# First mixing in one float32 matmul per group, and the last 64 keys of the values as one matmul per pair of heads

## Chip, cores and metric

The kernel runs on one core of a Trainium2 chip. The metric is device time in microseconds from launch to end, as the median of several executions. Inputs and outputs are float32.

## What is computed

Attention with talking heads, four batches of 12 heads, 448 positions and 64 channels a head, followed by a two-layer MLP without bias. `w_pre` mixes the heads of the scores before the softmax, `w_post` those of the probabilities behind it.

```python
scores = (1.0 / np.sqrt(64)) * np.matmul(q, k.transpose(0, 1, 3, 2))
scores = np.einsum('bhij,hg->bgij', scores, w_pre)
scores = scores - np.max(scores, axis=-1, keepdims=True)
attn = np.exp(scores)
attn = attn / (np.sum(attn, axis=-1, keepdims=True) + 1e-09)
attn = np.einsum('bhij,hg->bgij', attn, w_post)
x = np.matmul(attn, v)          # then (B, S, H * D): 1792 rows of 768
h = x @ w_in                    # 768 -> 2048
out = np.maximum(0.01 * h, h) @ w_out
```

## The kernel before

**Tiling.** The queries of a batch are cut into chunks of 120 rows (the last has 88), 16 chunks in all. A chunk is worked on in groups of 10 rows by 12 heads, so that 120 partitions hold one group with all its heads; there are 12 groups in a chunk of 120 rows and 9 in one of 88, 180 in all. Three groups of four make the steps `s` of a chunk, and each of the 12 steps `t` of the loop over chunks does one piece of every stage, for three chunks at once.

**Stages.** `scores(n, h)` makes the scores of one head on TensorE (PE): two float32r passes, with a high and a low part of the queries, into PSUM tile `pss`, which ScalarE (ACT) copies to `st`. `regroup` sends them by DMA into tiles `rt` of 120 partitions (10 rows by 12 heads). `softmax(n, s, g)` is the first mixing: VectorE (DVE) casts `rt` to float32r (`rhi`), GpSimd (POOL) subtracts to get the remainder (`rlo`; DVE does it for every fourth group), and three float32r passes with the matrix `kpre`, itself in a high and a low part, add up in PSUM tile `psm`, which has two buffers. DVE takes the row maximum (`stat`), ACT the exponential and its sum (`et`). `mix` is the second mixing, in float32, with the matrix `kp` that holds `w_post` over the row sums: for each group and each 128 keys one matmul into `psa`, and for the last 64 keys, two of 64 columns each, even heads into the lower half of the partitions and odd heads into the upper (`half`). DVE and ACT copy `psa` to `at` and `half`. `values(n, pair)` multiplies with V for two heads at a time: head e of the pair writes partitions 64 e and up of `psx`, three matmuls over 128 keys and one over the last 64 for each head, so eight per pair. V stands twice for the last 64 keys, in the lower and in the upper half of the partitions, because the host repeats them.

**Beside it.** `prep_k` and `prep_q` split keys and queries into high and low parts on DVE, ACT and POOL; the keys of the next batch come in the third chunk of each batch. `Narrow` turns the 64-bit weights of the MLP into float32 (ACT, DVE, POOL), 36 pieces during the attention and 28 at the start of the MLP. `load_v` fetches the V of a batch into the one buffer there is. The MLP then goes through the four batches in 16 blocks of the hidden layer, `hidden` into `psh` and `project` into `pso`, with three float32r passes per product.

**What sets the order.** All instructions are recorded in the order of the loops, and a scheduler, which simulates a timeline of its own, puts each engine's queue in an order; each queue then runs strictly in that order. Tiles come from pools with a fixed number of buffers, and a buffer's next user waits for the last reader. All loads and stores but some of the results are issued by SyncE (SP).

Of the kernel before, what the change touches and what calls it, by code (L numbers as in the profile page):

```python
# [8 lines left out]
F32 = mybir.dt.float32  # L9
F32R = mybir.dt.float32r  # L10
# [11 lines left out]
ROWS = 10  # L22
# [10 lines left out]
def kernel(  # L33
# [10 lines left out]
    nc = tc.nc  # L44
    B, P, NJ, H, D = v.shape
    S = k.shape[3]
# [4 lines left out]
    RH = ROWS * H  # L51
    SLOTS = 3 * NJ
    HALF = SLOTS // 2
    HP = P // 2
# [13 lines left out]
    def pools(st, side):  # L68
        def pool(name, bufs, **kw):
            return st.enter_context(tc.tile_pool(name=name, bufs=bufs, side=side, **kw))  # L70
        return pool

    const = ctx.enter_context(tc.tile_pool(name="const", bufs=1, side="left"))
# [41 lines left out]
    pool = pools(left, "left")  # L115
    p_v = pool("v", 1)
    p_r = pool("r", SLOTS)
    p_rs = pool("rs", 3)
    p_e = pool("e", 2 * NJ + 1)
    p_st = pool("st", 2)  # L120
    p_at = pool("at", 2)
# [1 line left out]
    pool = pools(psum, "left")  # L123
# [3 lines left out]
    pool = pools(right, "right")  # L127
# [4 lines left out]
    p_c = pool("c", 1)  # L132
    ps_s = pool("ps_s", 3, space=PSUM)

    kw_t, k_t, q_t, v_t, s_t, r_t, rs_t, e_t, kp_t, at_t, xo_t = ({} for _ in range(11))

    def load_k(b, h):
        t = p_raw.tile([P, S], F32, tag="k", name="kraw", bufs=6)
# [34 lines left out]
    def load_v(b):  # L173
        t = p_v.tile([P, NJ, H, D], F32, tag="v", name="vt")
        nc.sync.dma_start(t, v[b])
        v_t[b] = t

    def scores(n, h):
# [20 lines left out]
    def softmax(n, s, g):  # L199
        sg = chunks[n][3][s]  # L200
        kk = sg[g][1] * H
        if g == 0:
            e_t[n, s] = [], p_st.tile([RH, 3, NJ], F32, tag="st", name="stat")
        es, st = e_t[n, s]
        e = p_e.tile([RH, S], F32, tag="e", name="et")
        es.append(e)
        raw = r_t.pop((n, s, g))
        hi = p_rs.tile([RH, S], F32R, tag="hi", name="rhi")
        lo = p_rs.tile([RH, S], F32R, tag="lo", name="rlo")
        nc.vector.tensor_copy(hi[:kk], raw[:kk])  # L210
        (nc.vector if g == 3 else nc.gpsimd).tensor_sub(lo[:kk], raw[:kk], hi[:kk].bitcast(F32))  # L211
        ps = ps_m.tile([RH, 512], F32, tag="m", name="psm")
        for i, (w, x) in enumerate(((1, hi), (0, lo), (0, hi))):
            nc.tensor.matmul(ps[:kk, :S], kpre[w][:kk, :sg[g][1], :], x[:kk], start=i == 0, stop=i == 2)  # L214
        nc.vector.tensor_reduce(st[:kk, 0, g:g + 1], ps[:kk, :S], axis=AX.X, op=ALU.max, negate=True)  # L215
        nc.scalar.activation(  # L216
            e[:kk], ps[:kk, :S], AF.Exp, bias=st[:kk, 0, g:g + 1], accum_out=st[:kk, 1, g:g + 1]
        )
        if g < len(sg) - 1:
            return  # L220
        kp = p_st.tile([RH, NJ, H, ROWS], F32, tag="kp", name="kp")
        kp_t[n, s] = kp
        full = sum(r == ROWS for _, r in sg)
        for a, z, kk in ((0, full, RH), (full, len(sg), sg[-1][1] * H)):
            if a < z:
                rs = st[:kk, 2, a:z]
                nc.vector.tensor_scalar_add(rs, st[:kk, 1, a:z], 1e-9)
                nc.vector.reciprocal(rs, rs)
                nc.vector.tensor_mul(  # L229
                    kp[:kk, a:z].rearrange("p g h r -> p g (h r)"),  # L230
                    kpost[:kk].rearrange("p h r -> p (h r)").unsqueeze(1).broadcast_to([kk, z - a, RH]),
                    rs.unsqueeze(2).broadcast_to([kk, z - a, RH]),
                )
# [38 lines left out]
    def values(n, pair):  # L272
        b, i0, m, _ = chunks[n]
        at, half = at_t[n]
        if pair % 3 == 0:
            xo_t[n] = ps_x.tile([P, 4, P], F32, tag="x", name="psx")
        ps = xo_t[n]
        for c in range(NJ):
            for e in range(2):
                h = 2 * pair + e  # L280
                up = slice(P) if c < NJ - 1 else slice(HP * e, HP * e + HP)
                nc.tensor.matmul(  # L282
                    ps[D * e:D * (e + 1), pair % 3, :m], v_t[b][up, c, h, :],
                    at[:, c, h, :m] if c < NJ - 1 else half[up, pair, :m], start=c == 0, stop=c == NJ - 1,
                )
        if pair % 3 == 2:
            xo = p_x.tile([P, 3, CHUNK], F32, tag="xo", name="xo")
            nc.vector.tensor_copy(xo[:, :, :m], ps[:, :3, :m])
            xo_t[n, pair // 3] = xo
# [92 lines left out]
    wt = const.tile([RH, 2, H], F32, name="wt")  # L382
    for i, w in enumerate((w_pre, w_post)):
        nc.sync.dma_start(wt[:, i, :], w.unsqueeze(0).broadcast_to([ROWS, H, H]))
    kraw = const.tile([RH, ROWS, H], F32, name="kraw")
    kpre = [const.tile([RH, ROWS, H], F32R, name=f"kpre{i}") for i in range(2)]
    kpost = const.tile([RH, H, ROWS], F32, name="kpost")
    nc.vector.tensor_copy(kraw, wt[:, 0, :].unsqueeze(1).broadcast_to([RH, ROWS, H]))
    nc.vector.tensor_copy(kpost, wt[:, 1, :].unsqueeze(2).broadcast_to([RH, H, ROWS]))
    for t, pat in ((kraw, ((H, ROWS), (0, H))), (kpost, ((0, H), (H, ROWS)))):  # L390

        nc.gpsimd.affine_select(
            t, t, pattern=[[-a, z] for a, z in pat], base=0, channel_multiplier=1, compare_op=ALU.is_ge, fill=0.0
        )
        nc.gpsimd.affine_select(
            t, t, pattern=[[a, z] for a, z in pat], base=H - 1, channel_multiplier=-1,
            compare_op=ALU.is_ge, fill=0.0,
        )

    nc.vector.tensor_copy(kpre[0], kraw)  # L400
    nc.vector.tensor_sub(kpre[1], kraw, kpre[0].bitcast(F32))

    with tc.issue_after(behind.ins):
        load_q(1)
# [1 line left out]
    regroup(0, 0, SLOTS)  # L406
    ctx.enter_context(tc.issue_after(last_dma[0].ins))
    load_v(0)
    prep_q(1, nc.vector.tensor_copy)
    for g in range(NJ):  # L410
        softmax(0, 0, g)
# [3 lines left out]
    for n in range(NCK):  # L415
        b = chunks[n][0]
# [3 lines left out]
        for t in range(SLOTS):  # L420
            s, c = divmod(t, NJ)
# [4 lines left out]
            if t == 0 and n % NB == 1 and n > 1:  # L426
                load_v(b)
# [11 lines left out]
            if t >= HALF and n:  # L439
                values(n - 1, t - HALF)  # L440
            nxt = (n, s + 1) if s < 2 else (n + 1, 0)
            if nxt[0] < NCK and c < len(chunks[nxt[0]][3][nxt[1]]):
                softmax(*nxt, c)
# [35 lines left out]
    for pair in range(NPAIR):  # L479
        values(NCK - 1, pair)  # L480
# [4 lines left out]
    pool = pools(mlp, "left")  # L485
# [3 lines left out]
    for i in range(1, n + 1):  # L489
        b, f = divmod(i, NF)  # L490
# [61 lines left out]
```

## Time and profile before

| | |
|---|---|
| time, median of 3 executions | 1090.8 us (1083.04 to 1097.96) |
| span of the profiled execution, its own time | 1094.2 us |
| PE busy | 1012.1 us, 93% |
| DVE busy | 839.4 us, 77% |
| POOL busy | 444.6 us, 41% |
| ACT busy | 424.6 us, 39% |
| first pass of the second MLP matmul | starts at 616.78 us |

The page and the trace are of one execution. PE's busy time covers a pass from its start to the end of its tail, and passes overlap, so a busy PE can still have room; the start-to-start distance of passes is the better measure of what one costs. "PEclk" is the TensorE clock that was granted, as a share of 2.4 GHz. Idle time of an engine stands with the one that ended it.

### The profile page before, as it was taken

The numbers are of one execution on the slowest core, as the hardware profiler recorded it, in microseconds if no ns is written. First come the engines' busy times: TensorE is split into PE (matmuls) and PEld (weight loads), VectorE is DVE, ScalarE is ACT, GpSimd is POOL, SyncE is SP. The second block draws the span as 40 slices with busy tenths as digits, with TensorE's granted clock in tenths as the row PEclk, the third lists the DMA queues.
The fourth block names the chain that finished last, engine by engine and source line by source line (L and its number), as shares of the span: only waits on it lengthen the run. The fifth ranks groups of instructions, "written<-read, shape, count | busy, mean of one in ns | idle before, by whom it ended". The sixth has DMA issues, their size and how long they took to land. (4 is left out here: it accounts for less than half of the span.)

```text
span 1094.2 us, 17821 instructions
## 1 busy us (share of the span) xinstructions
PE 1012.1 (93%) x6564; PEld 842.9 (77%) x6564; DVE 839.4 (77%) x1390; ACT 424.6 (39%) x951; POOL 444.6 (41%) x356
## 2 busy tenths in 40 slices
PE   4899889997899999999999988889999999999998
PEld 2576667775777767677768777779999999999997
DVE  6899887789888999768797599997556755565553
ACT  3664365644645646455552233332112211121111
POOL 5677764578565676546441165661000000000000
PEclk9999889998999999899999999999999999999999
DMA  5746533764354624536263455566333634353421
GB/s 184 282 161 194 190 110 119 234 198 156 119 171 158 240 70 154 177 112 216 100 230 89 136 181 177 178 179 214 102 116 103 205 102 116 104 163 101 116 89 63
DMA packets 93771, 167.11 MB, mean 153 GB/s; under 512 B 26740, under 2 KB 68724, under 8 KB 93172
## 3 DMA queue, kind: packets, MB, share of 16 engines
q1 hardware_dynamic: 91956, 163.23, 47.0%
q10 hardware_dynamic: 1728, 2.75, 0.7%
q8 instruction: 51, 0.84, 0.3%
q14 instruction: 36, 0.29, 0.1%
HBM read 103.82 MB, written 23.59 MB: 116 GB/s over the span
## 5 line engine op out<-in xcount | busy, mean ns | idle before, releaser
L211 POOL TENSOR_TENSOR rlo<-rt,rhi 120x448 fp32r<-120x448 f32 x144 | 175.3, 1221 | 141.6 <-DVE rhi L210 82.2
L332 DVE CAST wh<-wr 128x768 fp32r<-128x768 f32 x128 | 88.7, 695 | 138.3 <-PE psh L339 88.4
L256 PEld LDWEIGHTS psa<-kp,et 120*128 120x128 f32 (+2 forms) x1800 | 166.0, 174 | 35.7 <-issue 18.2
L256 PE MATMUL psa<-kp,et 120*128 120x120 f32 (+2 forms) x1800 | 179.8, 262 | 13.2 <-DVE kp L229 9.4
L216 ACT ACTIVATE et<-psm,stat 120x448 f32<-120x448 f32 x180 | 114.7, 639 | 152.7 <-DVE stat L215 151.3
L214 PE MATMUL psm<-rhi,kpre 120*120 120x448 f32 x360 | 149.5, 420 | 22.0 <-ACT et L216 21.7
L339 PE MATMUL pso<-gh,wl 128*128 128x448 f32 x384 | 141.7, 371 | 14.0 <-DVE wl L333 13.4
L339 PE MATMUL psh<-xh,wl 128*128 128x448 f32 x384 | 140.6, 366 | 3.5 <-DVE g L351 3.5
L339 PE MATMUL pso<-gl,wh 128*128 128x448 f32 x384 | 141.4, 368 | 0.0
L339 PE MATMUL pso<-gh,wh 128*128 128x448 f32 x384 | 141.4, 368 | 0.0
L339 PE MATMUL psh<-xh,wh 128*128 128x448 f32 x384 | 140.6, 366 | 0.0
L339 PE MATMUL psh<-xl,wh 128*128 128x448 f32 x384 | 140.4, 366 | 0.0
L350 ACT ACTIVATE t<-psh 128x448 f32<-128x448 f32 x64 | 34.8, 544 | 252.5 <-PE psh L339 243.2
L210 DVE CAST rhi<-rt 120x448 fp32r<-120x448 f32 x180 | 129.0, 717 | 2.3 <-DMA rt<-st 2.3
L215 DVE TENSOR_REDUCE stat<-psm 120x1 f32<-120x448 f32 x180 | 110.4, 614 | 26.4 <-PE psm L214 26.2
L333 DVE TENSOR_TENSOR wl<-wr,wh 128x768 fp32r<-128x768 f32 x128 | 123.8, 968 | 1.6
L187 ACT ACTIVATE st<-pss 120x448 f32<-120x448 f32 (+1 forms) x192 | 97.1, 551 | 57.4 <-PE pss L186 27.4
L282 PE MATMUL psx<-at,vt 128*64 128x120 f32 (+1 forms) x1152 | 109.0, 282 | 4.1 <-DVE at L264 2.7
L214 PEld LDWEIGHTS psm<-rhi,kpre 120*120 120x120 f32 x360 | 68.9, 191 | 47.0 <-ACT et L216 31.9
L282 PEld LDWEIGHTS psx<-at,vt 128*64 128x64 f32 x1152 | 68.0, 141 | 43.8 <-issue 31.5
L186 PE MATMUL pss<-kst,qlo 128*120 128x448 f32 (+1 forms) x192 | 82.3, 428 | 20.1 <-POOL kst L146 10.2
L339 PEld LDWEIGHTS pso<-gh,wl 128*128 128x128 f32 x384 | 72.9, 190 | 24.1 <-issue 14.5
(64 smaller groups left out, 1658.7 us busy)
## 6 DMA issues: line engine op xcount, KB each, us to landing
wr<-w_dram SPq DMA_DIRECT2D x114, 384.0 KB
rt<-st SPq DMA_DIRECT2D x176, 210.0 KB
craw<-in_w_moe SPq DMA_DIRECT2D x64, 384.0 KB
kraw<-in_k SPq DMA_DIRECT2D x48, 224.0 KB
qraw<-in_q SPq DMA_DIRECT2D x11, 720.0 KB
w_dram<-w SPq DMA_DIRECT2D x36, 192.0 KB
vt<-in_v SPq DMA_DIRECT2D x4, 1536.0 KB
xr<-x_dram SPq DMA_DIRECT2D x24, 224.0 KB
```

The costliest lines, as they stand in the source:

```text
L186: nc.tensor.matmul(ps[:m, :S], w[:, h, :m], k_t[b, h], start=i == 0, stop=i == 1)
L187: nc.scalar.activation(s_t[n][:m, h, :], ps[:m, :S], AF.Copy, scale=scale)
L210: nc.vector.tensor_copy(hi[:kk], raw[:kk])
L211: (nc.vector if g == 3 else nc.gpsimd).tensor_sub(lo[:kk], raw[:kk], hi[:kk].bitcast(F32))
L214: nc.tensor.matmul(ps[:kk, :S], kpre[w][:kk, :sg[g][1], :], x[:kk], start=i == 0, stop=i == 2)
L215: nc.vector.tensor_reduce(st[:kk, 0, g:g + 1], ps[:kk, :S], axis=AX.X, op=ALU.max, negate=True)
L216: nc.scalar.activation(e[:kk], ps[:kk, :S], AF.Exp, bias=st[:kk, 0, g:g + 1], accum_out=st[:kk, 1, g:g + 1])
L256: nc.tensor.matmul(ps[p0:p0 + np, w * g:w * g + nh * r], es[g][:r * H, c * P:c * P + np], kp[:r * H, g, h::step, :r], start=True, stop=True,)
L282: nc.tensor.matmul(ps[D * e:D * (e + 1), pair % 3, :m], v_t[b][up, c, h, :], at[:, c, h, :m] if c < NJ - 1 else half[up, pair, :m], start= ...
L332: nc.vector.tensor_copy(hi, raw)
L333: nc.vector.tensor_sub(lo, raw, hi.bitcast(F32))
L339: nc.tensor.matmul(ps, w[a][:, c * P:(c + 1) * P], x[e], start=first and j == 0, stop=last and j == 2)
```

## The change

The first mixing becomes one float32 matmul per group, straight from the regrouped tile `rt` and with a float32 `kpre`; the cast, the subtraction, their tiles and the split of `kpre` go. In the values, V's last block is made block-diagonal: in the half of the partitions that belongs to the even head, the columns of the odd heads are cleared, and the other way round, by two POOL instructions behind each load of V. One matmul over all 128 partitions and 128 columns then gives both heads of a pair their last 64 keys. It comes first in the pair and opens the sum; the six matmuls over 128 keys follow.

```diff
@@ pools, load_v @@
-    p_rs = pool("rs", 3)
...
         nc.sync.dma_start(t, v[b])
+        for e in range(2):
+            nc.gpsimd.memset(t[HP * e:HP * (e + 1), NJ - 1, 1 - e::2, :], 0.0)
@@ softmax @@
         raw = r_t.pop((n, s, g))
-        hi = p_rs.tile([RH, S], F32R, tag="hi", name="rhi")
-        lo = p_rs.tile([RH, S], F32R, tag="lo", name="rlo")
-        nc.vector.tensor_copy(hi[:kk], raw[:kk])
-        (nc.vector if g == 3 else nc.gpsimd).tensor_sub(lo[:kk], raw[:kk], hi[:kk].bitcast(F32))
         ps = ps_m.tile([RH, 512], F32, tag="m", name="psm")
-        for i, (w, x) in enumerate(((1, hi), (0, lo), (0, hi))):
-            nc.tensor.matmul(ps[:kk, :S], kpre[w][:kk, :sg[g][1], :], x[:kk], start=i == 0, stop=i == 2)
+        nc.tensor.matmul(ps[:kk, :S], kpre[:kk, :sg[g][1], :], raw[:kk], start=True, stop=True)
@@ values @@
-        for c in range(NJ):
+        nc.tensor.matmul(
+            ps[:, pair % 3, :m], v_t[b][:, NJ - 1, 2 * pair:2 * pair + 2, :], half[:, pair, :m],
+            start=True, stop=False, skip_group_check=True,
+        )
+        for c in range(NJ - 1):
             for e in range(2):
                 h = 2 * pair + e
-                up = slice(P) if c < NJ - 1 else slice(HP * e, HP * e + HP)
                 nc.tensor.matmul(
-                    ps[D * e:D * (e + 1), pair % 3, :m], v_t[b][up, c, h, :],
-                    at[:, c, h, :m] if c < NJ - 1 else half[up, pair, :m], start=c == 0, stop=c == NJ - 1,
+                    ps[D * e:D * (e + 1), pair % 3, :m], v_t[b][:, c, h, :], at[:, c, h, :m],
+                    start=False, stop=c == NJ - 2, skip_group_check=True,
                 )
@@ constants @@
-    kpre = [const.tile([RH, ROWS, H], F32R, name=f"kpre{i}") for i in range(2)]
+    kpre = const.tile([RH, ROWS, H], F32, name="kpre")
...
-    nc.vector.tensor_copy(kpre[0], kraw)
-    nc.vector.tensor_sub(kpre[1], kraw, kpre[0].bitcast(F32))
```

With the instructions the scheduler's order changes too. On PE, in the values of the sixth chunk, this stood before (in brackets, the engines or DMA queues that an instruction waits for):

```order
L282 MATMUL psx<-at,vt 64x120 x6
L282 MATMUL psx<-half,vt 64x120 x2
L214 MATMUL psm<-rhi,kpre_251 120x448 [waits Activation_49]
L282 MATMUL psx<-at,vt 64x120 x6
L282 MATMUL psx<-half,vt 64x120 x2
L214 MATMUL psm<-rhi,kpre_251 120x448 [waits Activation_49]
L214 MATMUL psm<-rlo,kpre_250 120x448 [waits DVE_49]
L214 MATMUL psm<-rhi,kpre_250 120x448
```

And this stands there now; line numbers are four to eight lower from the first mixing on:

```order
L274 MATMUL psx<-half,vt 128x120 [waits DVE_49]
L281 MATMUL psx<-at,vt 64x120 x6
L210 MATMUL psm<-rt,kpre 120x448 [waits DMAHW3_49,Activation_49]
L274 MATMUL psx<-half,vt 128x120
L281 MATMUL psx<-at,vt 64x120
L252 MATMUL psa<-kp,et 128x120 [waits DVE_49,PE_49]
L252 MATMUL psa<-kp,et 128x120 x3
L281 MATMUL psx<-at,vt 64x120 x5
L210 MATMUL psm<-rt,kpre 120x448 [waits DMAHW4_49,Activation_49]
```

The last block of a pair stands in front of it instead of behind it, as one matmul of 128 partitions; the three passes of a first mixing are one matmul, and its wait for POOL or DVE is one for a DMA queue.

On DVE, in the third chunk, where the keys of the second batch are prepared, this stood before:

```order
L145 CAST kst<-kraw 128x448 [waits DMAHW1_49,PE_49]
L227 TENSOR_SCALAR stat<-stat 120x4 [waits Activation_49]
L215 TENSOR_REDUCE stat<-psm 120x1 [waits PE_49]
L210 CAST rhi<-rt 120x448 [waits Pool_49]
L228 RECIPROCAL stat<-stat 120x4 [waits DVE_49]
L145 CAST kst<-kraw 128x448 [waits DMAHW2_49,PE_49]
L145 CAST kst<-kraw 128x448 [waits DMAHW3_49,PE_49]
L211 TENSOR_TENSOR rlo<-rt,rhi 120x448 [waits DVE_49]
L229 TENSOR_TENSOR kp<-kpost,stat 120x480 [waits DVE_49]
L215 TENSOR_REDUCE stat<-psm 120x1 [waits PE_49]
```

And now:

```order
L223 TENSOR_SCALAR stat<-stat 120x4 [waits Activation_49]
L211 TENSOR_REDUCE stat<-psm 120x1 [waits DVE_49,PE_49]
L224 RECIPROCAL stat<-stat 120x4 [waits DVE_49]
L144 CAST kst<-kraw 128x448 [waits DMAHW2_49,PE_49]
L225 TENSOR_TENSOR kp<-kpost,stat 120x480 [waits DVE_49]
L260 COPY at<-psa 128x4x12x10 [waits PE_49]
L260 COPY half<-psa 128x4x6x10 [waits PE_49]
L144 CAST kst<-kraw 128x448 [waits DMAHW3_49,PE_49]
L211 TENSOR_REDUCE stat<-psm 120x1 [waits PE_49] x2
L287 COPY xo<-psx 128x360 [waits PE_49]
```

The casts and the remainder between the row maxima are gone, and the maxima stand one behind the other.

On POOL, between the narrowing and the low parts of the queries in the second batch, this stood before:

```order
L109 TENSOR_TENSOR w<-w,exp 128x384 [waits DMAHW5_49,DVE_49,Activation_49]
L110 TENSOR_TENSOR w<-w,top 128x384 [waits Pool_49]
L211 TENSOR_TENSOR rlo<-rt,rhi 120x448 [waits DMAHW2_49,DVE_49,PE_49]
L211 TENSOR_TENSOR rlo<-rt,rhi 120x448 [waits DMAHW5_49,DVE_49,PE_49]
L109 TENSOR_TENSOR w<-w,exp 128x384 [waits DMAHW7_49,DVE_49,Activation_49]
L211 TENSOR_TENSOR rlo<-rt,rhi 120x448 [waits DMAHW6_49,DVE_49,PE_49]
L110 TENSOR_TENSOR w<-w,top 128x384 [waits Pool_49]
L211 TENSOR_TENSOR rlo<-rt,rhi 120x448 [waits DMAHW7_49,DVE_49,PE_49]
L109 TENSOR_TENSOR w<-w,exp 128x384 [waits DMAHW2_49,DVE_49,Activation_49]
L170 TENSOR_TENSOR qlo<-qraw,qhi 128x6x90 [waits DMAHW3_49,PE_49,Activation_49]
```

And now:

```order
L109 TENSOR_TENSOR w<-w,exp 128x384 [waits DMAHW5_49,DVE_49,Activation_49]
L110 TENSOR_TENSOR w<-w,top 128x384 [waits Pool_49]
L109 TENSOR_TENSOR w<-w,exp 128x384 [waits DMAHW7_49,DVE_49,Activation_49]
L110 TENSOR_TENSOR w<-w,top 128x384 [waits Pool_49]
L176 MEMSET vt 64x6x64 [waits DMAHW2_49,PE_49]
L176 MEMSET vt 64x6x64 [waits Pool_49]
L109 TENSOR_TENSOR w<-w,exp 128x384 [waits DVE_49,DMAHW0_49,Activation_49,Pool_49]
L110 TENSOR_TENSOR w<-w,top 128x384 [waits Pool_49]
L169 TENSOR_TENSOR qlo<-qraw,qhi 128x6x90 [waits DMAHW6_49,PE_49,Activation_49]
L169 TENSOR_TENSOR qlo<-qraw,qhi 128x6x90 [waits Activation_49]
```

The subtractions are gone, and the clearing of V stands in the queue with a wait for V's transfer.

## Rows read from the trace of the kernel before

**Rows 1.** The page: span, and busy time of each engine.

```profile
span 1094.2 us, 17821 instructions
PE 1012.1 (93%) x6564; PEld 842.9 (77%) x6564; DVE 839.4 (77%) x1390; ACT 424.6 (39%) x951; POOL 444.6 (41%) x356
```

**Rows 2.** The chain that ended last: by line, and one block (start, us, what).

```profile
by line: PE pso L339 16.4%; PE psh L339 15.2%; issue 3.4%; DVE wh L332 1.6%; DVE wl L333 1.4%; DVE top L102 1.1%; POOL wr L109 0.8%; ACT wr L101 0.7%; DVE g L351 0.5%; DVE gl L353 0.4%; DVE top L105 0.4%; POOL wr L110 0.4%; ACT gh L352 0.4%
...
801.34 3.65 PE psh L339 x18
```

**Rows 3.** Windows: from:to, length, PE, PEld, DVE, ACT, POOL busy, clock, DMA.

```profile
60.00:600.00 540.00, 500.56 (x4032) 383.57 (x4032) 468.41 (x843) 287.62 (x682) 332.96 (x268) 0.96 0.48 160
116.00:126.00 10.00, 6.92 (x36) 5.79 (x36) 10.00 (x12) 4.75 (x9) 9.76 (x8) 0.51 0.60 207
130.00:140.00 10.00, 10.00 (x104) 8.50 (x103) 6.96 (x16) 2.98 (x8) 3.57 (x3) 1.00 0.78 263
...
259.00:270.00 11.00, 7.48 (x45) 4.63 (x46) 10.62 (x14) 3.32 (x9) 10.84 (x8) 0.53 0.50 168
...
617.00:744.00 127.00, 110.01 (x510) 97.02 (x510) 115.89 (x172) 44.73 (x91) 74.71 (x56) 0.97 0.60 182
```

**Rows 4.** Groups of instructions: line, engine, names, count | busy, mean ns | idle before.

```profile
L211 POOL TENSOR_TENSOR rlo<-rt,rhi 120x448 fp32r<-120x448 f32 x144 | 175.3, 1221 | 141.6 <-DVE rhi L210 82.2 <-PE pss L186 22.6 <-PE psm L214 12.8
...
L210 DVE CAST rhi<-rt 120x448 fp32r<-120x448 f32 x180 | 129.0, 717 | 2.3 <-DMA rt<-st 2.3
...
L211 DVE TENSOR_TENSOR rlo<-rt,rhi 120x448 fp32r<-120x448 f32 x36 | 25.2, 700 | 0.1
```

**Rows 5.** Timeline of PE, three stretches: start, us, instruction, idle before.

```profile
222.99 0.84 PE L282 MATMUL psx<-at,vt 128*64 128x120 f32 x12
223.76 0.47 PE L214 MATMUL psm<-rhi,kpre 120*120 120x448 f32 x1
...
225.66 2.04 PE L256 MATMUL psa<-kp,et 120*128 120x120 f32 x16
227.47 0.44 PE L214 MATMUL psm<-rhi,kpre 120*120 120x448 f32 x1
...
228.25 0.42 PE L282 MATMUL psx<-at,vt 128*64 128x120 f32 x2
228.60 0.42 PE L282 MATMUL psx<-half,vt 64*64 64x120 f32 x4
228.95 0.44 PE L186 MATMUL pss<-kst,qlo 128*90 128x448 f32 x1
...
615.27 0.68 PE L282 MATMUL psx<-at,vt 128*64 128x88 f32 x12
615.87 0.37 PE L282 MATMUL psx<-half,vt 64*64 64x88 f32 x4
616.78 0.47 PE L339 MATMUL pso<-gh,wl 128*128 128x448 f32 x1 [0.54 <-DVE xo L288]
```

**Rows 6.** Who waited for whom: us in total, times, longest.

```profile
ACT et L216 <- DVE stat L215: 151.3, 95, 10.2
...
PEld psm L214 <- ACT et L216: 31.9, 34, 4.7
```

**Rows 7.** Timeline of DVE and POOL, 138 to 142 us.

```profile
138.19 0.39 DVE L210 CAST rhi<-rt 120x448 fp32r<-120x448 f32 x1
...
140.65 1.15 POOL L211 TENSOR_TENSOR rlo<-rt,rhi 120x448 fp32r<-120x448 f32 x1 [0.51 <-DVE rhi L210]
...
140.96 1.08 DVE L210 CAST rhi<-rt 120x448 fp32r<-120x448 f32 x1
```

**Rows 8.** Timeline of ACT at 454 us.

```profile
454.38 1.42 ACT L187 ACTIVATE st<-pss 120x448 f32<-120x448 f32 x3 [4.34 <-DMA x_dram<-xo]
```

**Rows 9.** Timeline of DVE and PE at the start.

```profile
25.56 0.39 DVE L210 CAST rhi<-rt 120x448 fp32r<-120x448 f32 x1 [1.87 <-DMA rt<-st]
...
29.20 0.73 PE L214 MATMUL psm<-rlo,kpre 120*120 120x448 f32 x1 [0.20 <-POOL rlo L211]
```

More of the change, by code (lines that the diff above doesn't have):

```diff
@@ L133 @@
     ps_s = pool("ps_s", 3, space=PSUM)
-    kw_t, k_t, q_t, v_t, s_t, r_t, rs_t, e_t, kp_t, at_t, xo_t = ({} for _ in range(11))
+    kw_t, k_t, q_t, v_t, s_t, r_t, e_t, kp_t, at_t, xo_t = ({} for _ in range(10))
     def load_k(b, h):
@@ L384 @@
         nc.sync.dma_start(wt[:, i, :], w.unsqueeze(0).broadcast_to([ROWS, H, H]))
-    kraw = const.tile([RH, ROWS, H], F32, name="kraw")
-    kpre = [const.tile([RH, ROWS, H], F32R, name=f"kpre{i}") for i in range(2)]
+    kpre = const.tile([RH, ROWS, H], F32, name="kpre")
     kpost = const.tile([RH, H, ROWS], F32, name="kpost")
-    nc.vector.tensor_copy(kraw, wt[:, 0, :].unsqueeze(1).broadcast_to([RH, ROWS, H]))
+    nc.vector.tensor_copy(kpre, wt[:, 0, :].unsqueeze(1).broadcast_to([RH, ROWS, H]))
     nc.vector.tensor_copy(kpost, wt[:, 1, :].unsqueeze(2).broadcast_to([RH, H, ROWS]))
-    for t, pat in ((kraw, ((H, ROWS), (0, H))), (kpost, ((0, H), (H, ROWS)))):
+    for t, pat in ((kpre, ((H, ROWS), (0, H))), (kpost, ((0, H), (H, ROWS)))):
         nc.gpsimd.affine_select(
```

## The prediction

> **What bounds the kernel now.** I read four views in this order: the page, the chain that ended last, the windows, and the timeline of single stretches. The page gives a span of 1094.2 us, PE busy for 93% of it and DVE for 77% [rows 1]. The chain names only lines of the two MLP matmuls and of the narrowing work, none of the attention [rows 2]. So what the change can move is the moment at which the MLP may begin: the first pass of the second MLP matmul starts at 616.78 us, right behind the last values [rows 5]. Behind it lie 127 us in which DVE is busy for 116, with the narrowing and splitting of the weights [rows 3], and then blocks of 18 passes on PE, one behind the other, to the end [rows 2]. Neither contains an edited line, so I keep all 477 us. The whole question is what becomes of the first 617.
>
> In the steady attention, 60 to 600 us, PE is busy 500.6 of 540 us, DVE 468.4 and POOL 333.0, and the mean granted clock is 0.96 [rows 3]. Two engines are nearly full. The short windows tell which waits for which. From 130 to 140 DVE is 70% busy and PE has no gap. From 116 to 126 and from 259 to 270 DVE is full or nearly so; PE falls to 69% and 68% busy, and these are stretches at the lower level of the clock, 1.2 GHz, with a mean of 0.51 and 0.53 [rows 3]. These are the places where the keys of the next batch are prepared beside the softmax. The waits say the same: the exponential waited 151.3 us in all for the row maximum on DVE, and the first mixing's matmul waited on the exponential for its PSUM buffer [rows 6]. So PE sets the pace where DVE keeps up, and DVE sets it where it does not. The change loads the one and unloads the other.
>
> What this costs now: PE is idle for 540 - 500.6 = 39.4 us, and 0.04 x 540 = 21.6 us are lost by the lower clock. Together about 61 us, a little too much, since some idle time lies in the slow stretches. The busy figure on the other side covers waits shorter than a pass's tail, so I take 61 as it stands.
>
> **First mixing, on PE.** Before, each of the 180 groups has three float32r passes of 448 columns. From 227.47 to the next line's start at 228.25 is 0.78 us [rows 5], of which some 0.1 us is the step to the 64-column layout of the values; three passes without it are 18-pass blocks of the MLP by ratio: 3.65 / 18 = 0.203 us each [rows 2], 0.61 together. After, there is one float32 matmul. The trace has none of 448 columns, but it shows that a float32 matmul runs as two passes (a pair of the values has six full matmuls, and the trace twelve records), and what a pass costs by its length: 16 passes of 120 columns take 227.47 - 225.66 = 1.81 us, so 0.113 us each. The slope comes from the values: twelve records, which run as six pairs side by side, take 223.76 - 222.99 = 0.77 us with 120 columns and 615.87 - 615.27 = 0.60 us with 88 [rows 5]. That is 0.17 us / 6 / 32 = 0.9 ns a column, close to two clocks at 2.4 GHz (0.83 ns), where float32r takes one (187 of its 203 ns). With two clocks for each of 328 more columns a pass is 0.113 + 0.273 = 0.386 us, two are 0.77. The lower bound, if a long float32 pass ran as fast as a float32r one, is 0.41; the upper, by plain proportion to 120 columns, is 2 x 0.113 x 448 / 120 = 0.84. I take 0.77, since the slope is measured between two lengths of the same type. So PE gets 0.16 x 180 = 29 us more (bounds -36 and +41). This speaks against the change: four float32r-sized passes take the place of three.
>
> The Trainium skill prices this otherwise. FP8 and Floating Point Precision, TensorE Precision Notes, says that true FP32 is four passes through the array, and TensorE: Matmul & The Clock Gate, Back-to-back issue gap, gives N / 2.4 + 2.5 ns for a pass, an estimate of 189 ns with 448 columns. One pass more per group would then be 34 us. The trace has 203 ns for such a pass with its weight load, so the rows decide; the sum by the page would end 5 us later.
>
> **First mixing, on DVE and POOL.** 180 casts of 717 ns go, 129.0 us, and 36 subtractions on DVE, 25.2 us; on POOL 144 subtractions, 175.3 us [rows 4]. About 146 of DVE's 154 us lie between 60 and 600, which brings it from 468 to some 322 of 540, or 60%. That work lies on the path only where DVE is late. It also gets faster than the count says: the cast takes 0.39 us at 138.19, but 1.08 us at 140.96 beside a POOL subtraction [rows 7]. The Trainium skill, SBUF — State Buffer, SBUF: two separate sides, calls the port pair that both use an exclusive lock held for a whole instruction. The rows agree as far as they go; by that rule DVE's other two-input work would also shrink, which is the larger gain among the rivals.
>
> In the program's order PE no longer waits for POOL in front of a first mixing but for the DMA that brings the group. What is queued behind that wait is all of PE. I cost it at nothing: before, the cast on DVE waited for the same transfers, 2.3 us in all [rows 4]; the cover is the lead of several steps between regrouping and use. If it were gone, a late transfer would stop PE, at a few us each.
>
> **Recovered.** Of the 61 us, the bounds are 17 (only the two worst stretches: 3.1 us idle and 4.9 of clock from 116 to 126, 3.5 and 5.2 from 259 to 270, [rows 3]) and all 61. Not all of it is DVE's: at 454.38 ACT had waited 4.3 us for a transfer, with the exponentials behind it, and that stays [rows 8]. I take 45, nearer to the upper end, since DVE is 87% busy in the mean of all 540 us, and will be at 60%. At the start, the first group is there at 25.56 and its low part reaches PE at 29.20 [rows 9]; with neither cast nor subtraction I take 3 us off.
>
> **Values.** The last block of a pair costs 228.95 - 228.60 = 0.35 us, four records in a 64x64 layout of its own, with the entry into it [rows 5]. After, it is two passes of 0.113 in the full layout, and the entry into the 64-column layout of the rest, about 0.14, comes behind it. Where pairs follow one another that is 0.37, no gain; where a pair stands alone, in the middle of full matmuls, one change of layout goes and 0.12 is saved. 96 pairs give -12 to +2; I take -6. The clearing of V adds two POOL instructions per batch of 384 columns. Each is below the 1.22 us of a POOL subtraction [rows 4]. They wait for V's landing: 1.57 MB at the 160 GB/s of the steady part [rows 3] is an estimate of 10 us, in which POOL's queue stands, low parts of the queries and narrowing among it. Three times that, on an engine that will be idle for more than half the time, I cost at nothing; without cover it is up to 10 us each.
>
> **Sum.** +29 - 6 - 45 - 3 = -25. Against the profiled span that is 1069; it lies 3.4 us above the median of 1090.8, so the time I forecast is 1065 (bounds of this case 1050 to 1082).
>
> **Rivals.**
> 1. PE eats the gain, about 1094. The same 29 - 6 on PE, but only the 17 us of the two worst stretches come back, and the 3 us at the start. For it: in stretches like 130 to 140 PE has no gap [rows 3], and there each group simply costs 0.16 us more. Against it: DVE is 87% busy over the whole stretch, not only in the worst parts.
> 2. PE paces everything: 1113 or more. One mechanism: the waits that stop PE are released by transfers and ACT, as at 454.38 [rows 8], so DVE's relief returns nothing, and every float32 pass lies on the path; +29 + 2 on PE and a few us more from waits on regrouping transfers, which PE now meets itself. It is slower by 2% from the point where less than 8 us come back. Against it: the waits on DVE's row maximum are the longest of the attention [rows 6].
> 3. The full gain, about 1040. DVE and POOL stop slowing each other, no stretch falls to 1.2 GHz, and all 61 us come back, with -12 at the values: 29 - 12 - 61 - 3 = -47, and a few us from the shorter queue in front of each row maximum.
> 4. The float32 matmul does not cost what the slope says: at the lower bound of 0.41 us PE gains 36 us instead of losing 29, and the time is near 1000. Nothing in the rows speaks for it; the longer the float32 pass, the more columns would have to run at double pace.
>
> **How the numbers follow.** Forecast 0.50, rival 1 0.28, rival 2 0.08, rival 3 0.12, rival 4 0.02. The range leaves out rivals 2 and 4 and the far end of the others: 1038 to 1098. About 2% is what a measurement of this kernel can tell from no change, here 1069 and 1113. Of the forecast's 0.50 some 0.35 lie below 1069, with rivals 3 and 4 that makes 0.50 faster; 0.41 within 2%; 0.09 slower.
>
> **What would show it.** The first pass of the second MLP matmul should start near 592 instead of 616.78, and the 477 us behind it stay. First-mixing records: 360 instead of 540, started 0.38 to 0.39 us apart. DVE between 60 us and the end of the attention near 60%, POOL below 40%, and the stretches of key preparation at the full clock. If the mean clock stays at 0.96 and DVE's share falls all the same, rival 2's mechanism is at work. The forecast is wrong if float32 passes of 448 columns are not 0.39 us, or if PE's gaps turn out to be waits on transfers.

## The result, and the profile after

The changed kernel takes 1055.7 us (median of four, 1055.2 to 1056.3), beside 1090.8 us before (median of three, 1083.0 to 1098.0): ratio 0.9675, 95% interval 0.9631 to 0.9719. A fourth execution of the kernel before, 1101.4 us, is 1.7% above its fastest, counts as the chip's slower state, and is left out. That is some 35 us less; the forecast was 1065, some 26 us less. The two profiled executions, which the terms below are read from, lie 40.1 us apart (spans of 1094.2 and 1054.1), since that of the kernel before ran above its median.

The changed kernel's span and busy times, and the group of its first mixing (busy, mean ns, idle before; they answer to [rows 1] and [rows 4]):

```profile
span 1054.1 us, 16715 instructions
PE 1002.1 (95%) x6192; PEld 804.7 (76%) x6192; DVE 675.7 (64%) x1172; ACT 423.7 (40%) x951; POOL 266.2 (25%) x220
...
L210 PE MATMUL psm<-rt,kpre 120*120 120x448 f32 x360 | 174.3, 572 | 11.7 <-ACT et L212 8.1 <-DMA rt<-st 3.4
```

The windows, from 60 us to the end of the attention, the three stretches in which most casts of the next batch's keys (`kst`) now stand, and the narrowing behind the attention (columns as in [rows 3]):

```profile
60.00:576.50 516.50, 504.16 (x3798) 360.53 (x3796) 318.68 (x642) 285.08 (x678) 164.72 (x137) 1.00 0.50 169
99.00:115.00 16.00, 14.77 (x96) 9.56 (x96) 15.50 (x29) 9.12 (x23) 12.83 (x11) 1.00 0.43 121
230.00:244.00 14.00, 13.23 (x95) 8.34 (x93) 14.00 (x23) 8.74 (x21) 11.81 (x10) 1.00 0.42 116
365.00:378.00 13.00, 12.40 (x87) 7.90 (x87) 12.47 (x21) 7.82 (x21) 10.71 (x9) 1.00 0.20 61
577.00:704.00 127.00, 110.07 (x510) 96.80 (x509) 119.24 (x173) 44.76 (x91) 74.24 (x56) 0.97 0.60 183
```

PE is idle for 12.3 of 516.5 us; before, in the same stretch up to its end, for 40.6 of 556.7:

```profile
60.00:616.70 556.70, 516.12 (x4204) 396.75 (x4203) 474.68 (x854) 289.34 (x688) 332.96 (x268) 0.96 0.48 157
```

In the key preparation DVE is still full or nearly so (97%, 100% and 96%), but PE is busy for 92% to 95% and has the full clock. Before, key casts stand from 102 to 119 and from 246 to 261 us; the two stretches of [rows 3], with PE at 69% and 68% and a mean clock of 0.51 and 0.53, are the ends of these and what comes right behind. Over the whole attention from 60 us, DVE fell from 85% to 62%. The 127 us of narrowing are as they were, DVE busy for 119, PE 510 passes in both.

The waits answer to [rows 6] (PEld is the load of weights into PE):

```profile
ACT et L212 <- DVE stat L211: 93.2, 74, 5.4
...
PEld psm L210 <- ACT et L212: 14.6, 19, 2.1
```

The timeline of PE, at four places: the first mixing at the start, two later ones, and the end of the attention (as [rows 5, 9]):

```profile
25.55 1.85 PE L210 MATMUL psm<-rt,kpre 120*120 120x448 f32 x2 [3.43 <-DMA rt<-st]
...
42.68 1.67 PE L210 MATMUL psm<-rt,kpre 120*120 120x448 f32 x4
44.19 1.05 PE L252 MATMUL psa<-kp,et 120*128 120x120 f32 x8
...
211.47 0.92 PE L210 MATMUL psm<-rt,kpre 120*120 120x448 f32 x2
212.22 1.05 PE L252 MATMUL psa<-kp,et 120*128 120x120 f32 x8
...
575.32 0.68 PE L281 MATMUL psx<-at,vt 128*64 128x88 f32 x12
576.53 0.47 PE L338 MATMUL pso<-gh,wl 128*128 128x448 f32 x1 [0.54 <-DVE xo L287]
```

Two float32 passes take 212.22 - 211.47 = 0.75 us, four take 44.19 - 42.68 = 1.51, so some 0.376 each. The second MLP matmul begins at 576.53 instead of 616.78 us, 40.3 us earlier, and 477.6 us lie behind it as before: all of the change is in the attention.

Where in the attention, the thirteenth row maximum tells, the first of the second chunk. The view of one tile on DVE, of the kernel before and then of the changed one (durations in ns, first and last start in us):

```profile
L215 DVE TENSOR_REDUCE stat<-psm x13: 586/624/625, 30.3 to 64.6; 120x1 f32<-120x448 f32 x13
```

```profile
L211 DVE TENSOR_REDUCE stat<-psm x13: 608/624/625, 27.4 to 52.8; 120x1 f32<-120x448 f32 x13
```

It starts 11.8 us earlier, and the other 28.5 us come from there to the end of the attention. That divides the time and not quite the work, for the scheduler's new order puts this row maximum ahead of other work on PE. The windows up to it, before and now:

```profile
0.00:64.60 64.60, 43.61 (x176) 31.25 (x176) 51.59 (x75) 30.66 (x66) 39.40 (x36) 0.95 0.69 237
```

```profile
0.00:52.80 52.80, 35.17 (x132) 22.00 (x133) 30.41 (x49) 28.33 (x61) 22.38 (x23) 1.00 0.66 236
```

What PE had begun by then in the kernel before (54 passes of the scores, 14 first mixings, 80 records of the second mixing) the changed kernel has begun at some 55.5 us. By equal work it is about 9 us ahead there, and some 31 us come behind.

### The profile page after: what moved, and what is told of

The parts are those of the page before. It is cut to its first block, busy times and chain, and to the rows that moved or that the text cites. A ratio compares the mean times of both kernels' runs of the same rounds, so it can differ in the third digit from the quotient of the medians.

```text
span 1054.1 us, 16715 instructions
## 1 busy us (share of the span) xinstructions
PE 1002.1 (95%) x6192; PEld 804.7 (76%) x6192; DVE 675.7 (64%) x1172; ACT 423.7 (40%) x951; POOL 266.2 (25%) x220
## 4 chain that ended last, share of the span: by engine, by line
PE 49%; DVE 8%; issue 3%; DMA 2%; ACT 2%; POOL 1%; SPq 0%; ACTq 0%; DVEq 0%; POOLq 0%
PE psh L338 18%; PE pso L338 17%; PE psa L252 5%; PE psm L210 4%; PE psx L281 3%; DVE wh L331 2%; PE pss L187 2%; DVE wl L332 1%; DVE top L102 1%; PE psx L274 1%; DMA craw<-in_w_moe 1%; DVE top L105 1%; DVE gl L352 1%; DVE g L350 1%; ACT wr L101 1%
## 5 line engine op out<-in xcount | busy, mean ns | idle before, releaser
L252 PEld LDWEIGHTS psa<-kp,et 120*128 120x128 f32 (+2 forms) x1800 | 163.7, 170 | 55.6 <-issue 32.3
L210 PE MATMUL psm<-rt,kpre 120*120 120x448 f32 x360 | 174.3, 572 | 11.7 <-ACT et L212 8.1
L212 ACT ACTIVATE et<-psm,stat 120x448 f32<-120x448 f32 x180 | 114.1, 638 | 95.5 <-DVE stat L211 93.2
L187 PE MATMUL pss<-kst,qlo 128*120 128x448 f32 (+1 forms) x192 | 93.3, 486 | 13.8 <-POOL kst L145 10.0
L260 DVE COPY at<-psa 128x480 f32<-128x480 f32 (+2 forms) x112 | 68.3, 612 | 46.3 <-PE psa L252 45.8
L281 PE MATMUL psx<-at,vt 128*64 128x120 f32 (+1 forms) x1152 | 97.9, 273 | 0.0
L281 PEld LDWEIGHTS psx<-at,vt 128*64 128x64 f32 x1152 | 63.3, 137 | 36.9 <-issue 25.0
L169 POOL TENSOR_TENSOR qlo<-qraw,qhi 128x720 fp32r<-128x720 f32 (+1 forms) x30 | 59.0, 1985 | 102.3 <-ACT qhi L168 92.2
L210 PEld LDWEIGHTS psm<-rt,kpre 120*120 120x120 f32 x360 | 55.9, 184 | 34.5 <-ACT et L212 14.6
```

Source lines behind the costliest of these rows:

```text
L169: lo_op(to_lo, dealt, to_hi.bitcast(F32))
L187: nc.tensor.matmul(ps[:m, :S], w[:, h, :m], k_t[b, h], start=i == 0, stop=i == 1)
L210: nc.tensor.matmul(ps[:kk, :S], kpre[:kk, :sg[g][1], :], raw[:kk], start=True, stop=True)
L212: nc.scalar.activation(e[:kk], ps[:kk, :S], AF.Exp, bias=st[:kk, 0, g:g + 1], accum_out=st[:kk, 1, g:g + 1])
L252: nc.tensor.matmul(ps[p0:p0 + np, w * g:w * g + nh * r], es[g][:r * H, c * P:c * P + np], kp[:r * H, g, h::step, :r], start=True, stop=True,)
L260: copy(at[:, :, i:i + full * ROWS].rearrange("p h (g r) -> p g h r", r=ROWS), ps[:, :w * full].rearrange("p (g h r) -> p g h r", h=nh, r=R ...
```

## The experiments

Ratios are to the kernel before, timed beside each; the changed kernel's is 0.9675 (0.963 to 0.972). The kernel before had medians of 1090 to 1097 us, so where two experiments are compared, a difference of medians can be off by some us, and the ratios are the safer measure. Every edit also gives the scheduler's queues another order, which no run separates from the edit itself. The profiles are of one execution each.

**Each part alone: pre_only.** The values as before, V not cleared.

```diff
-        nc.tensor.matmul(ps[:, pair % 3, :m], v_t[b][:, NJ - 1, 2 * pair:2 * pair + 2, :], half[:, pair, :m], ...)
-        for c in range(NJ - 1):
+        for c in range(NJ):
             for e in range(2):
+                up = slice(P) if c < NJ - 1 else slice(HP * e, HP * e + HP)
...
```

> Only the first mixing is changed (one float32 matmul per group, no cast, no remainder); the values stand as before, with their four half-size passes per pair, and V is not cleared. If the gain comes from the first mixing, as my sum says, only the -6 us of the values are missing: about 1062 us (1056 to 1068), and the first pass of the second MLP matmul near 582 us instead of 576.5. If the full-size matmul of the values, which now opens each pair, is what took the gaps away, it is 1075 us or more.

1078.3 us (1070.1 to 1080.9), ratio 0.986 (0.979 to 0.993). Missed by 16 us, and by its median in the range that I gave to the other theory. The profile, of its fastest run (1070.1 us), speaks against that theory all the same: PE is idle for 12.0 of 530 us at the full clock, as in the changed kernel, so the gaps went without the full-size matmul.

```profile
60.00:590.00 530.00, 517.96 (x3991) 352.16 (x3989) 324.80 (x642) 285.97 (x678) 162.86 (x131) 1.00 0.49 164
```

There the thirteenth row maximum is at 52.8 us as in the changed kernel, and the end of the attention 13.4 us later; where the slower runs lose 8 us more isn't in any trace. In the timeline of PE:

```profile
223.68 0.62 PE L276 MATMUL psx<-at,vt 128*64 128x120 f32 x6
224.23 0.42 PE L276 MATMUL psx<-half,vt 64*64 64x120 f32 x2
224.58 1.01 PE L208 MATMUL psm<-rt,kpre 120*120 120x448 f32 x2
225.52 0.42 PE L276 MATMUL psx<-half,vt 64*64 64x120 f32 x2
225.87 0.44 PE L185 MATMUL pss<-kst,qlo 128*90 128x448 f32 x1
...
589.95 0.47 PE L333 MATMUL pso<-gh,wl 128*128 128x448 f32 x1 [0.54 <-DVE xo L282]
```

Here the scheduler splits the four small passes of a pair, and each half costs 0.35 us with its change of layout, as much as an undivided block in [rows 5]. But the timeline has 85 undivided blocks and only some 12 pairs in halves, so the splitting comes to 12 x 0.35 = 4 us. Added up from start to start, the values' records take 127.9 us of PE from 60 us on, and 120.3 in the changed kernel: 7.6 of the 13.4 us. The rest lies in the mixings and scores beside them.

**Each part alone: values_only.** The kernel before with the new values and the clearing; cast, remainder and three passes stay (the diff of the change without its part in `softmax`).

> Only the values are changed: block-diagonal V and one matmul per pair for the last 64 keys, with the two clearing instructions per batch on GpSimd; the first mixing stays with cast, remainder and three passes. By my sum it saves at most 12 us of PE work, of which little shows while VectorE is the late one: 1085 to 1094 us beside 1094. If the two parts share the gain, it is 1080 us or less.

1097.4 us beside 1096.6, ratio 1.004 (1.000 to 1.008). No gain, a little above the range that I gave and on its side. PE saved work and waited instead: up to the end of its attention it is idle for 51.2 us, where the kernel before had 40.6.

```profile
60.00:618.00 558.00, 506.83 (x4019) 406.71 (x4017) 481.70 (x855) 290.09 (x688) 332.57 (x274) 0.96 0.48 157
```

While DVE is late, PE time saved is worth nothing. By the ratios, the parts give 1.4% and nothing alone, and 3.3% together.

**The load without the wait: dead_both.**

```diff
         raw = r_t.pop((n, s, g))
+        hi = p_rs.tile([RH, S], F32R, tag="hi", name="rhi")
+        lo = p_rs.tile([RH, S], F32R, tag="lo", name="rlo")
+        nc.vector.tensor_copy(hi[:kk], raw[:kk])
+        (nc.vector if g == 3 else nc.gpsimd).tensor_sub(lo[:kk], raw[:kk], hi[:kk].bitcast(F32))
```

> The changed kernel, with the cast and the subtraction of each group put back on VectorE and GpSimd as they were, into tiles that nobody reads; the output is the same. TensorE waits for neither. If the load on VectorE and GpSimd was what cost the time, it comes back although nobody waits for the results: 1085 to 1110 us, VectorE near 85% busy in the attention, and the stretches of key preparation at 1.2 GHz again. If it was the chain from the cast over the remainder to the matmul, the time stays at 1065 us or less.

1111.1 us (1110.1 to 1111.6), ratio 1.015 (1.009 to 1.021). The whole gain is gone, although no matmul reads these tiles, and the rest is about what PE has more to do than before: 25.6 us in the first mixing less the values' 13. A window up to the end of its attention, its waits, and three groups:

```profile
60.00:630.70 570.70, 517.97 (x3844) 371.01 (x3844) 489.26 (x853) 290.62 (x690) 339.10 (x275) 0.98 0.46 153
```

```profile
ACT et L217 <- DVE stat L216: 179.9, 109, 7.2
...
PEld psm L215 <- ACT et L217: 49.9, 47, 4.3
```

```profile
L215 PE MATMUL psm<-rt,kpre 120*120 120x448 f32 x360 | 178.3, 583 | 39.0 <-ACT et L217 35.4 <-DMA rt<-st 3.4
...
L212 DVE CAST rhi<-rt 120x448 fp32r<-120x448 f32 x180 | 143.8, 811 | 7.0 <-DMA rt<-st 6.8
...
L145 DVE CAST kst<-kraw 128x448 fp32r<-128x448 f32 x42 | 32.4, 794 | 0.2
```

PE is idle for 52.7 us again, and the exponentials wait 180 us for row maxima. In front of the first mixings, where it was idle for 8.1 us behind exponentials, it is now for 35.4. The clock fell less than I expected: 0.98. The dead reads also hold the regrouped tiles longer, but PE does not wait for these: 3.4 us in front of the first mixings, in both kernels. What the longer hold does to other transfers was not separated.

**Only the cast: dead_cast.** As dead_both, without `rlo` and its subtraction.

> The changed kernel with the cast of each group put back on VectorE, into a tile that nobody reads, and without the subtraction. The cast alone is 0.39 us where nothing runs beside it, 70 us in 180 groups, which VectorE at 62% busy has room for: 1057 to 1066 us, and the cast's mean well below the 717 ns of the kernel before. If VectorE's count of instructions is the matter and not the company of GpSimd, it lies halfway to the kernel with both, 1070 us or more.

1070.2 us (1063.7 to 1073.9), ratio 0.977 (0.970 to 0.984), 14.5 us over the changed kernel by the medians, some 10 by the ratios, whose intervals touch. Neither answer: above my 1066 and at the 1070 that I gave the other theory, but a fifth to a quarter of the way to dead_both and not half. Its two groups:

```profile
L211 DVE CAST rhi<-rt 120x448 fp32r<-120x448 f32 x180 | 98.0, 560 | 22.4 <-DMA rt<-st 22.2
...
L145 DVE CAST kst<-kraw 128x448 fp32r<-128x448 f32 x42 | 28.7, 709 | 0.2
```

The same 180 casts take 46 us less than in dead_both, and those of the keys 3.7 less, with the subtractions gone, which were 34 us of DVE and 178 of POOL there. So of the 55 us that the dead work costs, some 10 to 15 come with the cast and about 40 with the subtractions and what they do to their neighbours. That 560 ns are still more than the 382 of the median goes with the other POOL work. Of the casts that its timeline lists singly, 84 run while POOL does nothing, at 0.38 us in the mean, and 32 beside a POOL instruction, at 0.99. In dead_both these are 24 at 0.38 and 104 at 0.94; row maxima, read from PSUM, are 0.61 to 0.62 either way.

**The start: dead_first.** As dead_both, under `if n == 0`, for the twelve groups of the first chunk.

> The changed kernel with cast and subtraction put back for the twelve groups of the first chunk only, into tiles that nobody reads. At the start the changed kernel is 12 us ahead by the twelfth row maximum, where my sum had 3. If VectorE's and GpSimd's work on these groups held up the start, 6 to 10 us come back: 1062 to 1066 us. If it was the way of the remainder to TensorE, which is not put back, the time stays at 1056 to 1058 us.

1063.6 us (1061.6 to 1070.4), ratio 0.977 (0.970 to 0.983): 8 us back, where the first theory said 6 to 10, though the interval overlaps that of the changed kernel. The thirteenth row maximum, and a window of the start:

```profile
L217 DVE TENSOR_REDUCE stat<-psm x13: 606/611/625, 29.4 to 61.1; 120x1 f32<-120x448 f32 x13
```

```profile
20.00:70.00 50.00, 38.93 (x196) 26.04 (x195) 41.01 (x64) 27.53 (x64) 29.29 (x24) 0.90 0.68 239
```

8.3 us later than in the changed kernel. (My expectation called it the twelfth.) Part of that goes with the clock, 0.90 in this window and 1.00 in the changed kernel's: no_clear (below), without any dead work, has the same 0.90 and this row maximum at 55.4.

```profile
L209 DVE TENSOR_REDUCE stat<-psm x13: 607/624/626, 27.3 to 55.4; 120x1 f32<-120x448 f32 x13
```

```profile
20.00:70.00 50.00, 40.23 (x204) 26.79 (x202) 27.23 (x52) 28.51 (x68) 17.84 (x14) 0.90 0.67 242
```

So 5.7 us are left for the dead work and the order that it brings. That the load on DVE and POOL holds up the start is likely, and not shown.

**PE's price: three_raw.**

```diff
-        nc.tensor.matmul(ps[:kk, :S], kpre[:kk, :sg[g][1], :], raw[:kk], start=True, stop=True)
+        for i, w in enumerate((1, 0, 0)):
+            nc.tensor.matmul(ps[:kk, :S], kpre[w][:kk, :sg[g][1], :], raw[:kk], start=i == 0, stop=i == 2)
```

> The changed kernel with three float32r passes per group, taken straight from the regrouped tile without cast or remainder: the low part of the scores is left out of the computation, so this is for its time alone. TensorE has 3 x 0.203 = 0.61 us per group instead of the 2 x 0.376 that the profile of the changed kernel shows, 26 us less in 180 groups; VectorE and GpSimd do the same as there. If TensorE paces the whole attention now, all 26 come off: 1030 us (1027 to 1036). If other waits stand behind it, less: 1045 us or more.

1044.0 us (1039.8 to 1046.6), ratio 0.957 (0.951 to 0.963): 12 us less than the changed kernel, not 26. The profile tells where the rest stayed. Its thirteenth row maximum, and its end of the attention in the timeline of PE:

```profile
L212 DVE TENSOR_REDUCE stat<-psm x13: 593/624/626, 26.7 to 61.4; 120x1 f32<-120x448 f32 x13
```

```profile
563.08 0.47 PE L339 MATMUL pso<-gh,wl 128*128 128x448 f32 x1 [0.54 <-DVE xo L288]
```

A window of the start, of three_raw and then of the changed kernel:

```profile
20.00:70.00 50.00, 37.21 (x195) 30.23 (x193) 26.68 (x48) 27.42 (x64) 18.32 (x15) 0.86 0.68 242
```

```profile
20.00:70.00 50.00, 41.74 (x228) 27.71 (x227) 29.04 (x55) 30.71 (x74) 19.12 (x17) 1.00 0.67 242
```

From the thirteenth row maximum to the end it takes 501.7 us, the changed kernel 523.7: 22 us less, or 19 if both are counted from the same amount of work on PE, which the changed kernel has begun at 55.5 us. PE saves 168 x 0.142 = 24 there, so it paces most of that stretch. The start is 8.6 us longer (6 by equal work), with PE busy for less of it and its clock at a mean of 0.86; neither theory had that. Here a start as late as dead_first's came without cast or subtraction, so a late start alone doesn't prove that they caused it.

**The clearing: no_clear.** Without the two `memset` in `load_v`.

> The changed kernel without the two instructions that clear half of V's last block; the heads of a pair then mix in the last 64 keys, so the output is another. I costed the clearing, with its wait for V's landing on GpSimd, at nothing: 1054 to 1057 us. If GpSimd's queue behind the wait (12.5 us in all by the waits) delays keys and queries, 1050 us or less.

1057.5 us (1056.5 to 1066.9), ratio 0.973 (0.965 to 0.981). The 2 us more are within the scatter of its own runs: leaving the clearing out gains nothing. In the changed kernel's groups, and then in its waits, it is 3.3 us of POOL and one long wait:

```profile
L176 POOL MEMSET vt<- 64x384 f32 x8 | 3.3, 412 | 12.7 <-DMA vt<-in_v 12.5
```

```profile
POOL vt L176 <- DMA vt<-in_v: 12.5, 3, 11.6
```

**The place of the full matmul: full_last.** The full matmul behind the six others, `start=c == 0` in these and `stop=True` in it.

> The changed kernel, with the full matmul of the last 64 keys behind the six half-width ones of its pair, where the four small passes stood before, and not in front of them. The values alone gave nothing, but without them the new first mixing is 1078 us (1070 to 1081). If their worth is the PE time of the 64x64 layout that is gone, its place in the pair does not matter: 1055 to 1060 us. If it is the place, since the last block of a chunk is the last to be copied and now the first to be asked for, the time goes back to 1065 us or more, or falls below 1052.

1061.4 us (1060.7 to 1063.5), ratio 0.975 (0.969 to 0.980). Between the two answers: 6 us more than in front, while without the full matmul it is 23 more. The intervals of 0.975 and 0.9675 overlap, so that the place matters is likely and not shown.

**More narrowing in the attention: early14, early14_lead, early6_lead, lead.** DVE has room now, and behind the attention it is still full. This is the edit of early14_lead; early14 has the new step but the old `narrowing.pop()()` under the old condition, without the lines behind it:

```diff
-EARLY = 2
+EARLY = 14
...
-            if (n * SLOTS + t) % 5 == 0 and pieces and not last:
+            if (n * SLOTS + t) % 3 == 0 and pieces and not last:
...
-            if (n * SLOTS + t) % 5 == 2 and narrowing:
-                narrowing.pop()()
+            if (n * SLOTS + t) % 3 == 2 and narrowing and (len(narrowing) > 1 or not pieces):
+                narrowing.pop(0)()
+            if n == NCK - 2 and t == SLOTS - 1:
+                while narrowing:
+                    narrowing.pop(0)()
```

> The changed kernel with 60 instead of 36 pieces of the weights narrowed during the attention, one in every third step instead of every fifth, and 4 instead of 28 at the start of the MLP. In 576 to 700 us VectorE is 97% busy and TensorE makes some 100 passes fewer than at 0.203 us each, about 20 us; during the attention VectorE has 62%, and the 24 pieces bring it some 36 us. If that room is real, 1035 us (1032 to 1045). If the attention pays it back in waits for row maxima, 1052 us or more.

> As the kernel that narrows 60 pieces during the attention (1068 us, one execution at 1048), but with each piece's transfer five steps ahead and not two. There the weights' stage was 14 us shorter, as expected, and the attention 26 us longer. If that came from ScalarE waiting for the transfers, it falls to 1045 us or less; if it is the work itself or the order that it brings, it stays at 1060 us or more.

> The milder form: 44 pieces during the attention, one in every fourth step, each fetched six steps ahead, and 20 at the start of the MLP. By the third that the eight pieces are of 24, some 5 to 7 us come off the start of the MLP: 1048 to 1052 us, if the attention has room for them; 1058 us or more if not.

> The changed kernel, with each piece of the weights narrowed five steps later than now, so that its 384 KB are fetched seven steps ahead and not two. ScalarE waits 46.5 us in all for these transfers between 40 and 570 us, with exponentials and copies queued behind, but TensorE has only some 20 us of gaps left: 1052 to 1057 us if they are covered, 1045 to 1050 if these waits are what is left of TensorE's gaps.

early14: four times of 1047.8, 1067.1, 1070.1 and 1071.2 us, too far apart for a ratio; the first is below the changed kernel. early14_lead: 1061.3 us (1055.1 to 1063.1), ratio 0.973 (0.967 to 0.979). early6_lead: 1057.6 us (1052.4 to 1060.6), 0.972 (0.965 to 0.978). lead: 1061.6 us (1057.1 to 1071.9), 0.976 (0.968 to 0.984). By its median none beats the changed kernel, and each missed the gain that was expected. In early14's profile (the execution of 1067.1 us, so what follows doesn't tell what the one of 1047.8 did), the end of the attention in the timeline, and two windows:

```profile
602.28 0.47 PE L338 MATMUL pso<-gh,wl 128*128 128x448 f32 x1 [0.54 <-DVE xo L287]
```

```profile
60.00:602.30 542.30, 516.00 (x3811) 366.71 (x3809) 361.50 (x716) 308.05 (x729) 215.18 (x187) 0.99 0.58 188
603.00:730.00 127.00, 126.40 (x612) 114.50 (x611) 80.73 (x123) 27.32 (x51) 10.11 (x8) 1.00 0.46 136
```

The narrowing stage gained the passes that were expected, 612 in 127 us instead of 510, and the time to the end fell from 477.6 to 463 us, 14.5 of the 20. The attention lost 25.8 us, with PE idle for 26 instead of 12. My other answer put such a loss on waits for row maxima, and these fell, from the 93.2 us shown above to 79.8. Fetching the pieces earlier took little off ScalarE's waits for them; between 40 and 570 us, in lead and then in the changed kernel:

```profile
ACT z L100 <- DMA craw<-in_w_moe: 43.7, 23, 3.7
```

```profile
ACT z L100 <- DMA craw<-in_w_moe: 46.5, 25, 3.3
```

So the kernels with a longer lead don't tell whether late transfers are the cause, since they hardly made them earlier in effect; whether it is that, the order or the work itself stays open.

## Why the prediction was right

Its mechanism held: PE pays for float32, and the relief of DVE and POOL gives back more. By its terms, with the changed kernel's profile against the one before (the rest worked out so that the sum closes at -40.3):

| term | forecast | measured | from |
|---|---|---|---|
| first mixing on PE | +29 | +25.6 | 180 x (0.752 - 0.61) |
| values | -6 | -13.4 | end of the attention against that of pre_only's fastest run |
| recovered, with the start | -45 - 3 | -52.5 | the rest: -40.3 - 25.6 + 13.4 |

The last row can be read from the other side too: between 60 us and the end, PE is idle for 40.6 - 12.3 = 28.3 us less, and the clock costs 0.04 x 556.7 = 22.3 us less (the clock is given to 0.01, so some 3 us either way), 50.6 in all. The division between the last two rows is less sure: by the ratios of pre_only and the changed kernel, the values are some 20 us and not 13.4, and the recovered time would be that much less. All three terms erred to the same side, 15 us together by the profiles.

**First mixing on PE: right.** A pass of 448 columns is 0.376 us, where the slope gave 0.386; both far from either bound, which answers the fourth rival as well. The Trainium skill's four passes (FP8 and Floating Point Precision, TensorE Precision Notes) agree in time with the new matmul, 0.752 / 4 = 0.188 us, though the trace has two records and not four; its sum was too high because the passes that go cost 0.203. three_raw shows that this price lies on the path: taken away, 19 to 22 us of it came off behind the start.

**Values: the size was off**, at -6 the lower bound of -12 would have been nearer. The values' own records fell by 7.6 us, close to -6; "where pairs follow one another that is 0.37, no gain" left out the dozen pairs that the scheduler splits, 4 us of it. The other 6 us and more lie with the neighbours on PE, which the term did not price. And it has no worth of its own: values_only shows that it came to nothing before DVE was relieved.

**Recovered: right in kind, a little small.** The 45 of 61 were for 60 us to the end, and the waits and the clock moved as forecast: idle time from 40.6 to 12.3 us, clock from 0.96 to 1.00. With DVE still full there, the stretches of key preparation now run at the full clock. What was too small is the start, 3 us for 11.8 at the thirteenth row maximum, or about 9 by equal work. I counted the way of one low part to PE. dead_first makes it likely that the load of cast and subtraction on all twelve groups counts, with 6 to 8 us; three_raw, as late without them, keeps that open.

**The rivals.** That PE eats the gain, or paces everything so that nothing comes back, both fell: dead_both puts 55 us of difference (52 by the ratios) on DVE's and POOL's load. The mechanism of the full gain, with no stretch of key preparation at 1.2 GHz, is nearly what happened; its 1040 took all 61 us. The 12.3 us of PE's idle time that stay are what it had too much.

**What would show it.** 576.5 against 592 for the end of the attention; 477.6 against 477 behind it; 360 records, 0.376 us apart against 0.38 to 0.39; DVE at 62% against 60%, POOL at 32% against less than 40%.

The time of dead_both is the measure of the theory: the same matmuls, none of which reads the dead tiles, and the gain gone, with PE waiting behind row maxima and exponentials. As instruction time the trace divides it: at the 0.38 and 0.61 us that cast and subtraction take beside an idle POOL, DVE's dead work would be 180 x 0.38 + 36 x 0.61 = 90 us, an estimate, and it took 143.8 + 34.0 = 178. The other 88 us are what DVE loses in POOL's company. How much of the 55 us on the path each of the two is worth, the experiments do not separate; dead_cast gives 10 to 15 us for the cast and about 40 for the subtractions with their company.

## What to carry to other kernels

A split into high and low parts that saves TensorE passes has a price on the engines that do the splitting. Where these set the pace, the plainer and longer matmul can win: here 0.14 us more per group on PE bought 0.7 us of cast and 1.2 us of subtraction. Price it per engine and ask which one is late, and after such a change ask again: savings on PE that were worth nothing before (the values) count behind it, and an engine at 62% is not therefore free for more work in the same stage.

## What was not expected of the hardware

A float32 pass of 448 columns, 0.376 us, costs less than two float32r passes of 448, 0.41, both at a granted clock of 1.00. It is within 1% of two clocks a column (0.373 us at 2.4 GHz), where a float32r pass has 16 ns on top of its 187.

The work of one engine changes the speed of another's: the same 180 casts on DVE took 811 ns in the mean with the subtractions on POOL and DVE, and 560 without. Singly, a cast takes 0.38 us while POOL does nothing and 0.94 to 0.99 beside a POOL instruction.
